# Two small tiles of a block-attention and mixture-of-experts kernel are made wider

## Chip, cores and metric

The kernel runs on one core of a Trainium2 chip. The metric is the device time of one execution in microseconds (us); the time before is the median of three runs. The five engines are TensorE (PE, its weight loads listed apart as PEld), VectorE (DVE), ScalarE (ACT), GpSimd (POOL) and SyncE (SP, which issues DMAs).

## What is computed

Block-causal attention (4 batches, 8 heads, 576 tokens, head size 64, blocks of 64), and behind it a mixture of four experts over the 2304 tokens, all in float32:

```python
scores = scale * np.matmul(q, k.transpose(0, 1, 3, 2))
mask = block_i >= block_j
scores = np.where(mask, scores, -1000000000.0)
attn = softmax of scores over the keys
x = (attn @ v), laid out as (2304, 512)
p = domain_probs / (domain_probs.sum(-1, keepdims=True) + 1e-09)
for e in range(4):
    h = np.maximum(x @ w1[e], 0.0)          # 512 -> 1024
    out += p[:, e:e + 1] * (h @ w2[e])      # 1024 -> 512
```

## The kernel before

The 2304 tokens are cut into five blocks: the first 64 tokens of all four batches (256), then the other 512 of each batch. A small planner in the kernel (`Flow`) gives every operation an engine, a cost in ns and a due time, and writes the program out in the order that it finds; the costs depend on sizes and engines alone, not on addresses.

To keep float32 precision every operand of a large product is split in two, a high part and the rest (`w1h`/`w1l`, `w2h`/`w2l`, `xh`/`xl`, `hh`/`hl`), and a product is three matmuls: high by high, rest by high, high by rest, each with its own weight load, 128 rows by 512 columns (256 for the first block).

- **First stage**, up to about 565 us: attention (scores at L521 and L522 from `KK`, `HH`, `LL`; the sums with `v` at L733 from `VN` and `S`) is worked in between the expert layers of the first three blocks. There the first layer is L1013 (`mm1`, moving `xh` or `xl`, stationary `w1h` or `w1l`) and the second L1063 (`mm2`, moving `w2h` or `w2l`, stationary `hh` or `hl`): 96 chunks, 12 first-layer matmuls each, and 960 matmuls of the second layer.
- **Last stage**, from about 565 us: the last two blocks go together through seven products instead of eight for each pair of chunks (`product`, L1236; moving are `xh`, `xl` and the sums `S1` to `S4` and `A22`, each with its high and rest part), ScalarE takes copies of products out of PSUM (L1256), and the second layer is L1299 (`mm2_half`).

All tiles lie one behind the other in each SBUF partition, in the order in which they are declared. The pool "const" holds what lives throughout: the weights' and activations' splits `w1h` ... `w2l`, `hh`, `hl`, `xh`, `xl`, the raw weights, and at its end `ident`, `probs_n` and `probs_s` (L284 to L287). The pool "attn" follows: `kr`, `qr`, `kT`, `qT`, `KK`, `HH`, `LL`, `VN`, `tr`, `tc`, then `S`, `cm`, `mx`, `sa`, `sb`, `xs`, `rc` (L289 to L310). Before the last stage "attn" is closed and the pool "pair" takes its place, from the same byte (L1114 to L1140): `A22`, `S2`, `S3`, `S1`, `S4`, more buffers for `hh`, `hl`, `w1h`, `w1l`, `w2h`, `w2l`, `w1r`, `o`, and `sc`. In a trace these buffers carry a p at the end of their names (`w2hp`, `hhp`, `scp`); `xh` and `xl` serve as `hh` and `hl` buffers too in this stage, as slices of a "const" tile.

The first tile, `w1h`, begins at byte 16,512 of the partition, which is 128 modulo 256. Every tile that TensorE reads is a multiple of 256 bytes long, and so are most others; `probs_n` has 320 bytes, `probs_s` 128, `tc` 64. So the offsets modulo 256 are:

```
                                   before
"const" tiles that TensorE reads      128
"attn": kr ... tr (KK, HH, LL, VN)     64     from byte 128,576
"attn": S ... rc                      128     from byte 170,880
"pair": all tiles                      64     from byte 128,576
```

Of the kernel before, what the change touches and what calls it, by code (L numbers as in the profile page):

```python
# [8 lines left out]
F32 = mybir.dt.float32  # L9
# [201 lines left out]
def kernel(  # L211
# [14 lines left out]
    P = 128  # L226
# [33 lines left out]
    MAXW = max(j[2] - j[1] for j in every)  # L260
# [3 lines left out]
    const = ctx.enter_context(tc.tile_pool(name="const", bufs=1))  # L264
# [4 lines left out]
    def bufs(tag, n, shape, dt=F32, pool=const):  # L269
        fl.add_bufs(tag, [pool.tile(shape, dt, name=f"{tag}{i}") for i in range(n)])  # L270
# [13 lines left out]
    XR = [const.tile([P, KC, MAXW], F32, name=f"xr{g}") for g in range(2)]  # L284
    ident = const.tile([P, P], F32, name="ident")
    probs_n = const.tile([P, len(BLOCKS) * 4, E], F32, name="probs_n")
    probs_s = const.tile([P, 32], F32, name="probs_s")  # L287
    const.seal()
    attn = short.enter_context(tc.tile_pool(name="attn", bufs=1))  # L289
    for tag, n, shape, dt in (  # L290
        ("kr", 2, [P, S], F32),
        ("qr", 1, [P, 2 * MAXW], F32),
        ("kT", 1, [P, S], F32),
        ("qT", 1, [P, 2 * MAXW], F32),
        ("KK", 2, [P, 2 * S], F32R),
        ("HH", 1, [P, 2 * MAXW], F32R),
        ("LL", 1, [P, 2 * MAXW], F32R),
        ("VN", 2, [P, (MASK_BLOCK + MAXW) // P + 1, 3, D], F32),
        ("tr", 1, [P, MAXW], F32),
        ("tc", 1, [P, MAXW // 32], F32),  # L300
        ("S", 2, [P, 2 * MAXC], F32),
        ("cm", 1, [P, 2 * MAXW], F32),
        ("mx", 1, [P, 2 * MAXW], F32),
        ("sa", 1, [P, 2 * MAXW], F32),
        ("sb", 1, [P, 2 * MAXW], F32),
        ("xs", 1, [P, MAXW], F32),
        ("rc", 1, [P, MAXW], F32),
    ):
        bufs(tag, n, shape, dt, attn)
        counts[tag] = n  # L310
# [1082 lines left out]
```

## Time and profile before

| | us |
|---|---|
| median of three runs | 908.78 (908.73 to 908.81) |
| the profiled execution, its own time | 909.63 |
| its span, first to last instruction | 907.6 |

The mean granted clock of TensorE over the span is 0.997. The profile lists an instruction as "line engine op out<-moving,stationary" for a matmul (the first name behind the arrow is what streams, the second what stands in the array); "128\*128 128x512 f32" is its shape. Matmuls are pipelined and the profile models their ends, so a matmul's duration is longer than the distance from its start to the next one's; the start times are what was recorded.

### The profile page before, as it was taken

Reading aid. Unit: us, or ns where it says so; the run is one execution under the profiler, and the core shown is the slowest. Engines: PE = TensorE matmul, PEld = TensorE weight load, DVE = VectorE, ACT = ScalarE, POOL = GpSimd, SP = SyncE. Lnnn points to the kernel's source line nnn. Section 1 sums busy time; section 2 is a strip of 40 time slices with the busy share of each in tenths; the row PEclk is TensorE's granted clock in tenths of the full one; section 3 lists DMA queues with packets and bytes.
Section 4 is the critical chain, followed back from the end, with each engine's and each line's share of the span. In section 5 each row is a group of like instructions: output and inputs, shape, how many; then the busy total and the mean of one; then the engine's idle time right before and its main releaser. Section 6 shows DMA issues by size and latency. Waiting matters only on the chain.

```text
span 907.6 us, 12364 instructions
## 1 busy us (share of the span) xinstructions
PE 896.4 (99%) x4302; PEld 714.6 (79%) x4302; DVE 692.5 (76%) x1298; ACT 451.3 (50%) x857; POOL 140.5 (15%) x53
## 2 busy tenths in 40 slices
PE   8999999999999999999999999899999999999998
PEld 4777888787877877787787787688888888888886
DVE  6799999888988988988988788965565655666532
ACT  3587766564646556557654643554343333333220
POOL 1101110422233142224232322000000000000000
PEclk9999999999999999999999999999999999999999
DMA  9875558455435345644444232312021212110002
GB/s 181 169 206 167 151 130 188 146 121 113 122 88 137 98 126 109 176 117 106 109 105 130 72 106 80 117 47 66 27 70 37 69 42 63 48 47 24 12 1 93
DMA packets 214654, 91.17 MB, mean 100 GB/s; under 512 B 130368, under 2 KB 195904, under 8 KB 214592
## 3 DMA queue, kind: packets, MB, share of 16 engines
q1 hardware_dynamic: 211424, 89.59, 38.0%
q10 hardware_dynamic: 3168, 0.79, 0.5%
q8 instruction: 34, 0.56, 0.3%
q14 instruction: 28, 0.23, 0.1%
HBM read 85.63 MB, written 4.72 MB: 100 GB/s over the span
## 4 chain that ended last, share of the span: by engine, by line
PE 92%; DVE 3%; DMA 2%; SPq 1%; ACT 0%; issue 0%; DVEq 0%; ACTq 0%
PE h L1013 23%; PE acc L1063 23%; PE acc L1299 20%; PE h L1236 9%; PE att L1236 7%; PE att L733 4%; PE att L521 2%; PE att L522 2%; SPq L339 1%; PE acc L733 1%; PE att L509 1%; DMA S<-in_v_dram 1%; DVE xr L352 1%; PE acc L509 1%; DMA probs_n<-in_moe_domain_probs_dram 0%; DMA cm<-in_q_dram 0%
## 5 line engine op out<-in xcount | busy, mean ns | idle before, releaser
L1013 PE MATMUL h<-xl,w1h 128*128 128x512 f32 (+1 forms) x384 | 136.5, 355 | 1.8 <-DVE xl L352 1.8
L1013 PE MATMUL h<-xh,w1h 128*128 128x512 f32 (+1 forms) x384 | 137.7, 359 | 0.0
L1013 PE MATMUL h<-xh,w1l 128*128 128x512 f32 (+1 forms) x384 | 136.6, 356 | 0.0
L1063 PE MATMUL acc<-w2h,hh 128*128 128x512 f32 x316 | 125.2, 396 | 0.0
L1063 PE MATMUL acc<-w2l,hh 128*128 128x512 f32 x316 | 123.5, 391 | 0.0
L1063 PE MATMUL acc<-w2h,hl 128*128 128x512 f32 x316 | 123.3, 390 | 0.0
L345 ACT CAST w2h<-w2r 128x512 fp32r<-128x512 f32 x113 | 70.3, 622 | 69.2 <-PE acc L1063 56.8
L666 POOL PARTITION_ALL_REDUCE sb<-sa x24 | 80.4, 3398 | 136.6 <-DVE sa L352 102.3
L687 POOL PARTITION_ALL_REDUCE mx<-cm x16 | 56.0, 3497 | 274.1 <-DVE cm L352 238.3
L352 DVE TENSOR_TENSOR w1l<-w1r,w1h 128x512 fp32r<-128x512 f32 (+1 forms) x124 | 86.7, 699 | 1.6 <-ACT w1h L345 0.6
L1030 ACT ACTIVATE hh<-h 128x512 fp32r<-128x512 f32 (+1 forms) x95 | 49.8, 525 | 72.1 <-PE h L1013 71.9
L352 DVE TENSOR_TENSOR w2l<-w2r,w2h 128x512 fp32r<-128x512 f32 x117 | 79.7, 682 | 4.9 <-ACT w2h L345 4.6
L1013 PEld LDWEIGHTS h<-xl,w1h 128*128 128x128 f32 x384 | 72.9, 190 | 12.6 <-DVE xl L352 2.2
L1013 PEld LDWEIGHTS h<-xh,w1h 128*128 128x128 f32 x384 | 72.9, 190 | 11.7 <-issue 1.2
L1013 PEld LDWEIGHTS h<-xh,w1l 128*128 128x128 f32 x384 | 72.9, 190 | 10.5
L345 ACT CAST w1h<-w1r 128x512 fp32r<-128x512 f32 (+1 forms) x111 | 66.1, 596 | 17.5 <-DMA w1r<-in_moe_w_dram 9.6
L1063 PEld LDWEIGHTS acc<-w2h,hl 128*128 128x128 f32 x316 | 59.3, 188 | 13.1
L1063 PEld LDWEIGHTS acc<-w2h,hh 128*128 128x128 f32 x316 | 59.5, 188 | 12.8 <-issue 1.7
L345 ACT COPY S<-att 128x512 f32<-128x512 f32 (+2 forms) x95 | 50.9, 536 | 34.4 <-DVE att L591 24.2
L1063 PEld LDWEIGHTS acc<-w2l,hh 128*128 128x128 f32 x316 | 59.5, 188 | 10.4
L1032 DVE SCALAR_TENSOR_TENSOR hl<-h,hh 128x512 fp32r<-128x512 f32 (+1 forms) x95 | 56.2, 591 | 10.5 <-ACT hh L1030 10.1
L352 DVE TENSOR_TENSOR S<-S,mx 128x1024 f32<-128x1024 f32 (+4 forms) x80 | 59.9, 792 | 3.2 <-POOL mx L687 3.0
(331 smaller groups left out, 1823.0 us busy)
## 6 DMA issues: line engine op xcount, KB each, us to landing
w2r<-in_moe_w_dram SPq DMA_DIRECT2D x128, 256.0 KB, 3.0
w1r<-in_moe_w_dram SPq DMA_DIRECT2D x120, 256.0 KB, 3.0
qr<-in_q_dram SPq DMA_DIRECT2D x112, 64.0 KB, 2.9
kr<-in_k_dram SPq DMA_DIRECT2D x64, 72.0 KB, 3.4
VN<-in_v_dram SPq DMA_DIRECT2D x32, 128.0 KB, 2.5
out_dram<-o SPq DMA_DIRECT2D x12, 256.0 KB, 2.1
w1rp<-in_moe_w_dram SPq DMA_DIRECT2D x8, 256.0 KB, 2.9
out_dram<-op SPq DMA_DIRECT2D x4, 256.0 KB, 2.0
```

The costliest lines, as they stand in the source:

```text
L345: o = op(engs, 0, lambda e: nc.scalar.copy(dst, src) if e == "act" else nc.vector.tensor_copy(dst, src), r, u, prio)
L352: o = op(engs, 0, lambda e: ENG[e].tensor_tensor(out=dst, in0=a, in1=b, op=alu), r, u, prio)
L509: nc.tensor.matmul(out=o, lhsT=KK.tile[hp, k0:k0 + n], rhs=qT.tile[hp, lo:W], start=True, stop=True)
L666: sums.append((yield op("pool", 150 + 6.3 * W, lambda _, h=h: nc.gpsimd.partition_all_reduce(sb.tile[:, h * W:h * W + W], sa.tile[:, h * W ...
L687: lambda _: nc.gpsimd.partition_all_reduce(mx.tile[:, :2 * W], src, P, RED.max),
L733: nc.tensor.matmul(out=x.tile[64 * g:64 * g + 64, W - w:W], lhsT=lhsT, rhs=rhs, start=(i == 0), stop=(i == len(todo) - 1))
L1013: nc.tensor.matmul(out=ps[:, :n], lhsT=s.tile[:, ks], rhs=x.tile[:, kc, :n], start=(kc == 0 and m == 0), stop=(kc == KC - 1 and m == 2),)
L1030: a = yield op("act", 0.833 * n + 55, lambda _: nc.scalar.activation(hh.tile[:, :n], ps[:, :n], AF.Relu), [mm], [pb, hh], 0.0)
L1032: l = yield op("dve", 1.04 * n + 70, lambda _: nc.vector.scalar_tensor_tensor(out=hl.tile[:, :n], in0=ps[:, :n], scalar=0.0, in1=hh.tile[: ...
L1063: nc.tensor.matmul(out=acc, lhsT=s.tile[:, ts], rhs=w.tile, start=(f == 0 and m == 0), stop=(f == FC - 1 and m == 2))
L1236: nc.tensor.matmul(out=ps[:, :n], lhsT=w.tile[:, ks], rhs=x[:, kc, :n], start=(start and kc == 0 and m == 0), stop=(i in (2, 3, 4) and kc ...
L1299: nc.tensor.matmul(out=acc, lhsT=s.tile[:, ts], rhs=w.tile, start=(c == 0 and x == 0), stop=(c == 3 and x == 2))
```

## The change

`probs_s` gets 48 columns instead of 32, and `tc` MAXW // 8 = 64 columns instead of 16. Both are read and written in the same slices as before; nothing else differs.

```diff
     probs_n = const.tile([P, len(BLOCKS) * 4, E], F32, name="probs_n")
-    probs_s = const.tile([P, 32], F32, name="probs_s")
+    probs_s = const.tile([P, 48], F32, name="probs_s")
     const.seal()
...
         ("tr", 1, [P, MAXW], F32),
-        ("tc", 1, [P, MAXW // 32], F32),
+        ("tc", 1, [P, MAXW // 8], F32),
         ("S", 2, [P, 2 * MAXC], F32),
```

## Rows read from the trace of the kernel before

**Rows 1.** The page: busy time of each engine, and the chain that ended last

```profile
PE 896.4 (99%) x4302; PEld 714.6 (79%) x4302; DVE 692.5 (76%) x1298; ACT 451.3 (50%) x857; POOL 140.5 (15%) x53
...
PE 92%; DVE 3%; DMA 2%; SPq 1%; ACT 0%; issue 0%; DVEq 0%; ACTq 0%
```

**Rows 2.** Stages from 565 us: busy PE, PEld, DVE, ACT, POOL; clock, DMA, GB/s

```profile
565.00:582.00 17.00, 14.38 (x61) 10.80 (x60) 17.00 (x25) 8.06 (x13) 0.00 (x0) 1.00 0.32 108
582.00:700.00 118.00, 118.00 (x512) 95.80 (x511) 72.83 (x132) 49.13 (x86) 0.00 (x0) 1.00 0.19 56
...
800.00:896.00 96.00, 96.00 (x418) 78.23 (x417) 48.46 (x81) 26.90 (x46) 0.00 (x0) 1.00 0.09 28
```

**Rows 3.** PE groups, 560 to 908 us: count | busy us, mean ns | idle before

```profile
L1299 PE MATMUL acc<-w2h,hhp 128*128 128x512 f32 x80 | 31.5, 394 | 0.0
...
L1299 PE MATMUL acc<-w2h,hlp 128*128 128x512 f32 x80 | 31.3, 392 | 0.0
...
L1299 PE MATMUL acc<-w2l,xh 128*128 128x512 f32 x60 | 23.5, 391 | 0.0
L1299 PE MATMUL acc<-w2lp,xh 128*128 128x512 f32 x44 | 17.4, 395 | 0.0
...
L1236 PE MATMUL att<-xh,w1hp 128*128 128x512 f32 x24 | 9.5, 394 | 0.0
...
L1299 PE MATMUL acc<-w2hp,hhp 128*128 128x512 f32 x24 | 9.4, 391 | 0.0
...
L1236 PE MATMUL att<-xh,w1l 128*128 128x512 f32 x24 | 9.3, 389 | 0.0
...
L1299 PE MATMUL acc<-w2hp,hh 128*128 128x512 f32 x20 | 7.9, 394 | 0.0
...
L1236 PE MATMUL h<-S3l,w1h 128*128 128x512 f32 x16 | 6.3, 396 | 0.0
...
L1236 PE MATMUL h<-A22h,w1h 128*128 128x512 f32 x16 | 6.3, 394 | 0.0
...
L1236 PE MATMUL h<-S3l,w1hp 128*128 128x512 f32 x16 | 6.3, 392 | 0.0
```

**Rows 4.** Timeline of PE near the end: start us, duration us, what

```profile
887.08 0.39 PE L1299 MATMUL acc<-w2h,xh 128*128 128x512 f32 x1
...
889.80 0.39 PE L1299 MATMUL acc<-w2hp,xh 128*128 128x512 f32 x1
...
892.60 0.39 PE L1299 MATMUL acc<-w2h,xh 128*128 128x512 f32 x1
...
900.78 0.39 PE L1299 MATMUL acc<-w2hp,hhp 128*128 128x512 f32 x1
...
903.28 0.39 PE L1299 MATMUL acc<-w2hp,hlp 128*128 128x512 f32 x1
```

**Rows 5.** The chain that ended last, in order of time: start, length us

```profile
583.77 7.00 PE h L1236 x30
```

**Rows 6.** Weight loads, 560 to 908 us: count | busy us, mean ns | idle

```profile
L1299 PEld LDWEIGHTS acc<-w2l,xh 128*128 128x128 f32 x60 | 11.3, 188 | 2.5
...
L1299 PEld LDWEIGHTS acc<-w2lp,xh 128*128 128x128 f32 x44 | 8.3, 188 | 1.9
```

**Rows 7.** DVE groups, 560 to 908 us: count | busy us, mean ns | idle

```profile
L352 DVE TENSOR_TENSOR w2l<-w2r,w2h 128x512 fp32r<-128x512 f32 x20 | 13.7, 687 | 4.2 <-ACT w2h L345 4.2
...
L352 DVE TENSOR_TENSOR w2lp<-w2r,w2hp 128x512 fp32r<-128x512 f32 x11 | 7.6, 688 | 7.0 <-ACT w2hp L345 6.9
```

**Rows 8.** One PE group, in 150 to 300 us and in 549 to 565 us

```profile
L1063 PE MATMUL acc<-w2l,hh 128*128 128x512 f32 x91 | 35.5, 390 | 0.0
...
L1063 PE MATMUL acc<-w2l,hh 128*128 128x512 f32 x12 | 4.7, 389 | 0.0
```

**Rows 9.** PE groups by shape, 60 to 545 us

```profile
L733 PE MATMUL att<-S,VN 128*64 128x448 f32 x52 | 12.0, 539 | 0.0
...
L733 PE MATMUL att<-S,VN 128*64 128x320 f32 x52 | 9.2, 432 | 0.0
```

## Prediction

> **What bounds the kernel now.** I read the busy times and the chain of waits first. TensorE is busy 99% of the span and carries 92% of the chain that ended last [rows 1]: nothing else has to get faster for the end to move, and no other engine can hide a gain of TensorE for long. Then the stage table. From 582 us on TensorE is busy for the whole of each stretch, at a granted clock of 1.00 (its 2.4 GHz level), while DVE, ACT and the DMA share fall off [rows 2]. Only 565 to 582 us has gaps (14.38 us busy of 17.00). So in the last third the time is the number of matmuls times the distance from one start to the next, and the question is what sets that distance.
>
> The distance can be read from start times. In the quiet end of the kernel twelve matmuls that read `w2h`/`w2l` against `xh`/`xl` start at 887.08 and the next group starts at 889.80: 2.72 us, 226.7 ns each. The next twelve, of the same shape, line and stationary tiles but with `w2hp`/`w2lp` moving, take 889.80 to 892.60: 2.80 us, 233.3 ns each. Nothing waits in either. Twelve more with both operands in p-tiles run from 900.78; the twelfth starts at 903.28, so 2.50 us over eleven, 227.3 ns [rows 4]. The chain of waits has a longer run of the slow kind at 583.77, thirty matmuls in 7.00 us, 233.3 ns each, these of the `S2` and neighbouring tiles against `w1h`/`w1l` [rows 5].
>
> The group table of the stage shows that this is general. A matmul's modelled duration moves with that distance, so the differences of the means count, not the means: `w2lp` against `xh` 395 ns, `w2l` against `xh` 391; `w2h` against `hhp` 394 and against `hlp` 392; `w2hp` against `hhp` 391; `S3l` against `w1h` 396, against `w1hp` 392; `xh` against `w1hp` 394, against `w1l` 389 [rows 3]. The slow ones are those whose two operands come from different pools. By the allocation, all tiles of the pool "const" begin at 128 modulo 256, and those of the pools "attn" up to `tc` and "pair" at 64. So **the pairs that cost more are those whose moving and stationary tile stand at different offsets modulo 256**. Equal offsets, 64 with 64 or 128 with 128, cost the same within about 1 ns.
>
> **What the change does, part by part.** `probs_s` grows from 128 to 192 bytes per partition: everything after it moves up by 64, so `kr` to `tr` and, later, all "pair" tiles go from 64 to 128. `tc` grows from 64 to 256 bytes: `S` to `rc` move by 256 in all and stay at 128. The two tiles are read and written in the same slices, so no instruction, wait, DMA or byte is added, removed or reordered; the planner's costs don't see an address. Only the offsets change.
>
> Now the sum, by classes of the two lines of the last stage, L1236 with 672 and L1299 with 768 matmuls. Their counts are those of the groups [rows 3]:
> - Moving at 64, stationary at 128: on L1299 three groups of 44 and three of 20, on L1236 24 groups of 16 or 8, 288 in all (`S3l` and `A22h` against `w1h` stand for them, 396 and 394). Together 480. Price of one: 4 ns by the means (395 against 391) to 6.6 ns by the quiet end (233.3 against 226.7). I take 5, nearer to the means, since they hold the whole stage with its other engines' traffic: 480 x 5 = 2.4 us (1.9 to 3.2).
> - Moving at 128, stationary at 64: on L1299 three groups of 80, on L1236 96 in six groups (one stands there, 394 against 389 with `w1l`). Together 336. Price 1 to 5 ns by these rows (392 and 394 against 391, 394 against 389), I take 2.5: 0.84 us (0.3 to 1.7).
> - Both at 64: 72 on L1299 and 192 on L1236, 264. Price 0 to 1 ns (391 and 392 against 391), I take 0.5: 0.13 us (0 to 0.26).
> - Both at 128 already: 360, nothing.
>
> That is 3.4 us. The 61 matmuls in 565 to 582 us [rows 2] are in these counts, and there TensorE stands waiting for ACT's copies of its own products, so what it saves is partly waited away: at 5 ns on about 40 of them, 0.2 us off. Left: **3.2 us**.
>
> The cover of a gain: who could become late next? In 582 to 896 us no stretch has idle TensorE, and DVE is busy 72.83 of 118.00 us in the first of these stretches and 48.46 of 96.00 in the last [rows 2]; a stage that runs 1% faster asks 1% more of engines that are a third idle. The output after the last matmul stays as long as it is.
>
> The weight loads aren't what is slow: 188 ns for one from `xh` under moving `w2lp` and 188 under `w2l` [rows 6]. VectorE doesn't see the offset either: its subtraction into `w2lp` takes 688 ns, into `w2l` 687 [rows 7]. So I cost the edit at nothing for the other engines.
>
> Before 565 us the two layers' 2,112 matmuls (by the loops) read "const" tiles alone and stay where they are. The attention's score products have both operands at 64 and will have both at 128: equal before and after, 0. Its products with `VN` (64) against `S` (128) are an unequal pair, in 4-byte float: between 320 and 448 columns their mean grows by 539 - 432 = 107 ns [rows 9], which is two cycles a column at 2.4 GHz with no excess that these rows can show. I take 0; at the quiet end's 6.6 ns for each of 160 pairs that run side by side it would be 1.1 us, which goes to the second rival below.
>
> The profiled execution took 909.63 us (span 907.63), 0.85 us over the median; the terms are differences and carry over. 908.78 - 3.2 = **905.6 us**; an execution like the profiled one would have a span near 904.4.
>
> **The rule that speaks against it.** The rows show 6.6 ns between two runs that differ in the moving tile's pool alone [rows 4]. The Trainium skill, page "TensorE: Matmul & The Clock Gate", section "Step-by-step: what each phase is for", has two independent read ports of SBUF, one for the moving operand and one for the weights, so that loading the next weights takes nothing from the running matmul. By it no pair of offsets could cost anything, and the sum would be 0 instead of 3.2 us. The trace differs: the price hangs on the pair, since `w2hp` moving is slow against `xh` and not against `hhp` [rows 3].
>
> **The rivals.**
> *Nothing changes (908.8 us).* Pool and offset go together in the kernel before, so the price may belong to where the pools lie, low and high in the partition, or to how these tiles are filled, and the offset is only its mark. Then all stays. For it: no row has a "const" tile at 64. Against it: `A22h` begins at byte 128,576, right behind the last "const" tile, and against `w1h` costs the same 394 ns as `w2hp`, 64 KB further up, does against `hh` [rows 3]; and `w2h` and `xh`, both "const" and some 40 to 60 KB apart, run at 226.7 ns [rows 4], so distance alone costs nothing. The Trainium skill's two read ports, above, would end here as well. To the same end leads that the allocator rounds sizes so that nothing moves; its tile of 64 bytes moved `S` by just 64, which speaks against it.
> *More than forecast (902.7 us).* Every matmul reaches the quiet end's pace: 480 x 6.6 + 336 x 4 + 264 x 2 = 5.0 us, and `VN` pairs give 1.1. Against it: equal pairs of the stage itself stand at 391 beside 389 in quieter stretches.
> *Slower (914 us).* What costs may be the coincidence of offsets between TensorE's reads and what VectorE, ScalarE and the DMAs do at the same time. Then moving the attention's tiles onto 128 puts them where the 2,112 early matmuls read. At the 4 ns of the means that is 8.4 us, less 3.2: 914. It decides from 3.2/2,112 = 1.5 ns on. Against it: those engines walk through whole tiles and pass every offset, and early groups run at 390 ns beside the attention's work and at 389 after it has ended [rows 8], so all they cost now is about 1 ns.
>
> **How the numbers follow.** Forecast 0.78, more than forecast 0.05, nothing changes 0.13, slower 0.04. The forecast's own terms, low and high, add to 2.0 and 5.0 us: 903.8 to 906.8; widened by 0.3 for the difference between executions (the profiled one stands 0.85 from the median, the three runs within 0.08 of each other) that is 903.5 to 907.1, and with the nearer half of the second case it holds 8 in 10. A change of 0.2% (1.8 us, 907.0) is about what can be told from none. Faster by more: nearly all of the forecast and the second case, 0.80; within: 0.15; slower: 0.05.
>
> **What would show it.** Right: `w2lp` against `xh` and `S3l` against `w1h` fall from 395 and 396 to 391 or less; `w2h` against `hhp` from 394 to 391; the twelve of `w2hp` against `xh` near the end take 2.72 us instead of 2.80; the stage from 582 us to the last matmul is 3 us shorter; weight loads stay at 188, subtractions at 687; the stretch up to 565 us ends within 0.5 us of where it did. Wrong: p-tile groups keep 394 to 396 (place, not offset), or the early groups rise above 390 (coincidence with the other engines), or TensorE shows idle time after 582 us.

## The result, and the profile after

The changed kernel takes 902.38 us (median of six), the kernel before 909.08 beside it: 6.7 us less, and the ratio of the two is 0.9916 (95% interval 0.9906 to 0.9926). The forecast was 905.6 us with a range of 903.5 to 907.1. The direction and the mechanism were right; the gain was twice the forecast of 3.2 us, and the time lies below the range. The rival "more than forecast" (902.7), which had been given a chance of 0.05, names the time that came.

The profiled execution after took 903.51 us, its span 901.6. The page: busy times, and the chain that ended last.

```profile
PE 890.2 (99%) x4302; PEld 715.3 (79%) x4302; DVE 692.3 (77%) x1298; ACT 451.8 (50%) x857; POOL 140.6 (16%) x53
...
PE 93%; DVE 3%; DMA 2%; SPq 1%; issue 0%; ACT 0%; DVEq 0%; ACTq 0%
```

The same 4,302 matmuls, and 6.2 us less of busy TensorE than in [rows 1]; every other engine is as busy as before. Where the time went is seen in the groups of the last stage, 560 to 908 us (count | busy us, mean ns | idle before):

```profile
L1299 PE MATMUL acc<-w2h,hhp 128*128 128x512 f32 x80 | 31.1, 389 | 0.0
...
L1299 PE MATMUL acc<-w2l,xh 128*128 128x512 f32 x60 | 23.3, 389 | 0.0
L1299 PE MATMUL acc<-w2lp,xh 128*128 128x512 f32 x44 | 17.1, 389 | 0.0
...
L1299 PE MATMUL acc<-w2hp,hhp 128*128 128x512 f32 x24 | 9.3, 389 | 0.0
...
L1236 PE MATMUL att<-xh,w1l 128*128 128x512 f32 x24 | 9.3, 389 | 0.0
...
L1236 PE MATMUL h<-S3l,w1h 128*128 128x512 f32 x16 | 6.2, 389 | 0.0
```

Beside [rows 3] the reader is to see two things. The unequal pairs fell from 394 to 396 ns, as forecast. But the equal ones fell too: `w2l` against `xh`, both at 128 in either kernel, from 391 to 389, and `w2hp` against `hhp` from 391 to 389. All stand now at the one value that `xh` against `w1l` had in the kernel before.

The weight loads are untouched, as in [rows 6]:

```profile
L1299 PEld LDWEIGHTS acc<-w2l,xh 128*128 128x128 f32 x60 | 11.3, 188 | 2.3
...
L1299 PEld LDWEIGHTS acc<-w2lp,xh 128*128 128x128 f32 x44 | 8.3, 188 | 1.7
```

The timeline gives the length of the last stage. Before, its first matmul on L1236 starts at 564.95 and its last on L1299 at 903.28 [rows 4]: 338.3 us.

```profile
564.95 0.39 PE L1236 MATMUL att<-xh,w1h 128*128 128x512 f32 x1
```

After:

```profile
564.71 0.39 PE L1236 MATMUL att<-xh,w1h 128*128 128x512 f32 x1
...
883.88 0.39 PE L1299 MATMUL acc<-w2hp,xh 128*128 128x512 f32 x1
...
886.60 0.39 PE L1299 MATMUL acc<-w2h,xh 128*128 128x512 f32 x1
...
897.25 0.39 PE L1299 MATMUL acc<-w2hp,hlp 128*128 128x512 f32 x1
```

That is 332.5 us, 5.8 less, and the twelve of `w2hp` against `xh` take 886.60 - 883.88 = 2.72 us, where [rows 4] had 2.80. The stage before it saved 0.9 us (below). 5.8 + 0.9 is the whole difference of the medians.

### The profile page after: what moved, and what is told of

Its sections match the earlier page's. It is cut to its first block, busy times and chain, and to the rows that moved or that the text cites. A ratio compares the mean times of both kernels' runs of the same rounds, so it can differ in the third digit from the quotient of the medians.

```text
span 901.6 us, 12364 instructions
## 1 busy us (share of the span) xinstructions
PE 890.2 (99%) x4302; PEld 715.3 (79%) x4302; DVE 692.3 (77%) x1298; ACT 451.8 (50%) x857; POOL 140.6 (16%) x53
## 4 chain that ended last, share of the span: by engine, by line
PE 93%; DVE 3%; DMA 2%; SPq 1%; issue 0%; ACT 0%; DVEq 0%; ACTq 0%
PE h L1013 24%; PE acc L1063 23%; PE acc L1299 19%; PE h L1236 9%; PE att L1236 7%; PE att L733 4%; PE att L521 2%; PE att L522 2%; PE att L509 1%; PE acc L733 1%; DMA w1r<-in_moe_w_dram 1%; SPq L339 1%; DMA S<-in_v_dram 1%; PE acc L509 1%; DVE xr L352 1%; DMA cm<-in_q_dram 0%
## 5 line engine op out<-in xcount | busy, mean ns | idle before, releaser
L1013 PE MATMUL h<-xl,w1h 128*128 128x512 f32 (+1 forms) x384 | 136.5, 356 | 1.9 <-DVE xl L352 1.9
L1013 PE MATMUL h<-xh,w1h 128*128 128x512 f32 (+1 forms) x384 | 137.5, 358 | 0.0
L1013 PE MATMUL h<-xh,w1l 128*128 128x512 f32 (+1 forms) x384 | 136.5, 355 | 0.0
L1063 PE MATMUL acc<-w2h,hh 128*128 128x512 f32 x316 | 125.1, 396 | 0.0
L1063 PE MATMUL acc<-w2l,hh 128*128 128x512 f32 x316 | 123.4, 391 | 0.0
L1063 PE MATMUL acc<-w2h,hl 128*128 128x512 f32 x316 | 123.2, 390 | 0.0
L1013 PEld LDWEIGHTS h<-xl,w1h 128*128 128x128 f32 x384 | 73.1, 190 | 12.4 <-DVE xl L352 2.1
L1013 PEld LDWEIGHTS h<-xh,w1h 128*128 128x128 f32 x384 | 72.9, 190 | 11.6 <-issue 1.2
L1013 PEld LDWEIGHTS h<-xh,w1l 128*128 128x128 f32 x384 | 73.0, 190 | 10.3
L1063 PEld LDWEIGHTS acc<-w2h,hl 128*128 128x128 f32 x316 | 59.3, 188 | 13.0
L1063 PEld LDWEIGHTS acc<-w2h,hh 128*128 128x128 f32 x316 | 59.5, 188 | 12.7 <-issue 1.7
L1063 PEld LDWEIGHTS acc<-w2l,hh 128*128 128x128 f32 x316 | 59.5, 188 | 10.3
```

The source lines that it names most:

```text
L1013: nc.tensor.matmul(out=ps[:, :n], lhsT=s.tile[:, ks], rhs=x.tile[:, kc, :n], start=(kc == 0 and m == 0), stop=(kc == KC - 1 and m == 2),)
L1063: nc.tensor.matmul(out=acc, lhsT=s.tile[:, ts], rhs=w.tile, start=(f == 0 and m == 0), stop=(f == FC - 1 and m == 2))
```

## The experiments

The theory after this result: a matmul whose moving and stationary tiles begin at different offsets modulo 256 is slow, and the equal ones that follow it are slow for a while too. The rivals: the offset itself (128 good, 64 bad); the place of the pools; the tiles from `S` on, which `tc` moves; other engines at work on tiles at 64.

Single executions of one kernel differ by up to 5.7 us (the kernel before, 907.67 to 913.36 in the 25 executions beside e5 to e7), and in the profiles the same matmul near 80 us starts anywhere between 78.2 and 81.5. Behind that point the stretches of kernels with the same distances between their tiles repeat to less than 0.1 us, so beside the time the table gives two stretches from the start times of each profile: from one first-layer matmul near 80 us (L1013) to the first matmul on L1236, and from there to the last on L1299. Each ratio is to executions of the kernel before taken beside the run (medians 910.12 us for e1 to e4, 909.67 for e5 to e7).

| kernel | offsets modulo 256 | time, us | ratio to before | near 80 us to L1236 | last stage |
|---|---|---|---|---|---|
| before | const 128, attn and pair 64 | 909.08 | | 485.42 | 338.34 |
| after | all 128 | 902.38 | 0.9916 | 484.49 | 332.54 |
| e1_probs_only | all 128, `S` to `rc` 192 | 903.29 | 0.9926 (0.9911 to 0.9941) | 484.49 | 332.59 |
| e2_tc_only | as before, `S` to `rc` 64 | 911.08 | 1.0009 (0.9999 to 1.0018) | 485.45 | 338.42 |
| e3_all_at_64 | all 64 | 903.53 | 0.9934 (0.9917 to 0.9950) | 484.49 | 332.59 |
| e4_w2_at_64 | as after, const `w2h`, `w2l` 64 | 913.26 | 1.0035 (1.0024 to 1.0047) | 490.33 | 336.98 |
| e5_pair_32 | as after, pair 160 | 909.65 | 1.0000 (0.9985 to 1.0015) | 484.49 | 339.19 |
| e6_pair_64 | as after, pair 192 | 909.03 | 0.9981 (0.9968 to 0.9994) | 484.49 | 338.35 |
| e7_pair_128 | as after, pair 0 | 908.14 | 0.9981 (0.9967 to 0.9996) | 484.49 | 338.34 |
| e8_w2p_only | as after, `w2hp`, `w2lp` 64 | 904.58, one execution | | 484.49 | 335.15 |
| e9_pair_256 | as after, pair 128 (384 modulo 512) | 902.58, one execution | | 484.49 | 332.53 |
| e10_w1p_only | as after, `w1hp`, `w1lp` 64 | 905.38, one execution | | 484.49 | 333.18 |

From the matmul near 80 us on, all of them have the same matmuls in the same order; only addresses differ. The unused tiles that make the distance are declared on the lines that are there already, so line numbers stay.

**Each half of the change alone.**

```diff
-    probs_s = const.tile([P, 32], F32, name="probs_s")
+    probs_s = const.tile([P, 48], F32, name="probs_s")
```

> One part alone: probs_s is widened, tc is not. The attention's tiles up to tr and all pair tiles go to 128 modulo 256, S to rc go to 192. Theory (the price lies on matmuls whose moving and stationary tile differ in offset, and equal pairs that follow them pay too): the whole gain, 902.4 us give or take 0.5, with every group of the last stage at 389 ns; S at 192 against VN at 128 costs nothing, since these products showed no price at 128 against 64 either. Rival (the price lies on S, sa and their neighbours): less than half of the gain, 906 or more.

```diff
-        ("tc", 1, [P, MAXW // 32], F32),
+        ("tc", 1, [P, MAXW // 8], F32),
```

> The other part alone: tc is widened, probs_s is not. S to rc go to 64, everything else stays as in the kernel before. Theory of the pair: no gain, 909 us, p-tile groups against const tiles at 394 to 396 ns as before. Rival (S, sa and neighbours carry the price): a gain of 3 us or more.

The first has the whole gain, both stretches to 0.05 us; the second has none. So `S` and its neighbours carry nothing: at 192 against `VN` at 128 (e1) or at 64 against 64 (e2) the stretches don't move. The change would have done with its first line.

**All at 64.** In the changed kernel:

```diff
-    bufs("w1h", 4, [P, DM], F32R)
+    const.tile([P, 48], F32, name="pad0"); bufs("w1h", 4, [P, DM], F32R)
```

> The changed kernel with 192 unused bytes ahead of the first tile: every tile that TensorE reads begins at 64 modulo 256 instead of 128. Theory of the pair: only the difference counts, so 902.4 us as the changed kernel, 389 ns throughout the last stage. Rival (the offset itself counts, 64 is the bad one): all 3,500 matmuls of the expert layers pay at least the 3 ns that pairs of 64 with 64 paid in the last stage of the kernel before (229.6 ns from start to start against 226.7), more than 10 us, 912 or more.

Both stretches are those of the changed kernel. The groups, 560 to 908 us:

```profile
L1299 PE MATMUL acc<-w2h,hhp 128*128 128x512 f32 x80 | 31.1, 389 | 0.0
...
L1299 PE MATMUL acc<-w2lp,xh 128*128 128x512 f32 x44 | 17.1, 389 | 0.0
...
L1236 PE MATMUL h<-S3l,w1h 128*128 128x512 f32 x16 | 6.2, 389 | 0.0
```

64 isn't a bad offset; what counts is that the two are equal. It also settles what the price of pairs 64 with 64 was in the kernel before: not theirs, but their neighbours'.

**Const tiles made unequal.** In the changed kernel:

```diff
-    bufs("w2h", 4, [P, DM], F32R)
+    const.tile([P, 48], F32, name="pad0"); bufs("w2h", 4, [P, DM], F32R)
     bufs("w2l", 4, [P, DM], F32R)
-    bufs("w1r", 3, [P, KC, P])
+    const.tile([P, 16], F32, name="pad1"); bufs("w1r", 3, [P, KC, P])
```

> The changed kernel with w2h and w2l of the const pool alone at 64 modulo 256 (192 unused bytes ahead of them, 64 behind), all else at 128. Theory of the pair: the second layer of the first three blocks, 960 matmuls that were fast in both kernels, becomes unequal and pays 6.6 ns each, 6.3 us; the first-layer groups behind them pay some 20 ns each for the way back, about 1.3 us; in the last stage 504 matmuls with w2h or w2l moving pay 3.3 us and their followers 0.5: 913.8 us, L1063 at 395 ns or more. Rival (the price belongs to where the pools lie in the partition, not to the offset): nothing, 902.4.

The time is 913.26 us, slower than the kernel before. The second layer of the first three blocks, fast in both kernels (390 ns in [rows 8]), became slow, and the first layer behind it too, whose own tiles had not moved (389 in the changed kernel). The groups of 300 to 450 us, and the second of them in the changed kernel:

```profile
L1063 PE MATMUL acc<-w2l,hh 128*128 128x512 f32 x92 | 36.3, 395 | 0.0
...
L1013 PE MATMUL h<-xl,w1h 128*128 128x512 f32 x89 | 34.8, 391 | 0.0
```

```profile
L1013 PE MATMUL h<-xl,w1h 128*128 128x512 f32 x92 | 35.8, 389 | 0.0
```

The stretch from 80 us to L1236 is 5.8 us longer than in the changed kernel, the last stage 4.4 us (expected 3.8). The first part fell short: 870 of the 960 second-layer matmuls lie in that stretch, and they take 4.6 us more, 5.3 ns each and not 6.6, the first layer 1.1 us more. Beside e1 and e3 (903.29 and 903.53), which run as the changed kernel does, 913.26 us is some 9.9 us more where 11.4 were expected, so that the nearness to 913.8 is partly luck. The place of a pool is out all the same: these are const tiles, low in the partition.

**How far apart.** In the changed kernel, an unused tile of 8, 16, 32 or 64 floats ahead of the pair pool:

```diff
-        more = ctx.enter_context(tc.tile_pool(name="pair", bufs=1, reuse_waits="tile"))
+        more = ctx.enter_context(tc.tile_pool(name="pair", bufs=1, reuse_waits="tile")); more.tile([P, 8], F32, name="pad0")
```

> The changed kernel with 32 unused bytes ahead of the pair pool: all tiles of the pair pool at 160 modulo 256, the const tiles at 128, a difference of 32. Theory (any difference of the two operands costs): unequal pairs at 233 ns from start to start and their followers slowed, the last stage as long as in the kernel before, 908 to 909 us. Rival (the price grows with the difference): about half of it, 905.5.

> The same with 64 unused bytes: pair tiles at 192, const tiles at 128, a difference of 64 in the other direction than in the kernel before. Theory: as the kernel before, 908 to 909 us. Rival (only tiles that begin below the other's offset pay): 902.4.

> The same with 128 unused bytes: pair tiles at 0, const tiles at 128 modulo 256. If what counts is the offset modulo 256: unequal pairs at 233 ns, 908 to 909 us. If it is the offset modulo 128, or 64: 902.4 us as the changed kernel, 389 ns throughout the last stage.

> The changed kernel with 256 unused bytes ahead of the pair pool: pair tiles at 384 modulo 512, const tiles at 128, equal modulo 256 and unequal modulo 512. If what counts is the offset modulo 256: the last stage as in the changed kernel, 332.5 us from its first to its last matmul, 389 ns throughout. If it is modulo 512 or more: 338 us as in the kernel before.

The last stage is 339.2, 338.4 and 338.3 us at distances of 32, 64 and 128 bytes, and 332.5 at 256. The price doesn't grow with the distance, it is paid to either side, and equality modulo 256 is enough to be rid of it. One group of this view in 560 to 908 us, at 32, at 128 and at 256 bytes:

```profile
L1299 PE MATMUL acc<-w2lp,xh 128*128 128x512 f32 x44 | 17.4, 395 | 0.0
```

```profile
L1299 PE MATMUL acc<-w2lp,xh 128*128 128x512 f32 x44 | 17.3, 394 | 0.0
```

```profile
L1299 PE MATMUL acc<-w2lp,xh 128*128 128x512 f32 x44 | 17.1, 389 | 0.0
```

At 64 bytes the equal length of the stage hides a change: the two unequal classes have changed places. In the kernel before, where the pair tiles lie 64 below the const tiles, the mean distance from start to start is 233.2 ns for a pair tile moving against a const tile and 230.9 ns the other way round; in e6, where they lie 64 above, it is 230.9 and 233.2. At 32 bytes both are at 233 (233.0 and 233.1), which is most of the 0.8 us by which that stage is longer than in the kernel before; at 128 bytes, where above and below are the same modulo 256, both are at 232.4 to 232.5. So at a distance of 64 the price depends on the side: a moving tile 64 below its stationary tile costs more than one 64 above.

**One unequal moving tile, and who pays behind it.** In the changed kernel:

```diff
-        add("w2h", 2, [P, DM], F32R)
+        more.tile([P, 48], F32, name="pad0"); add("w2h", 2, [P, DM], F32R)
         add("w2l", 2, [P, DM], F32R)
-        add("w1r", 1, [P, KC, P])
+        more.tile([P, 16], F32, name="pad1"); add("w1r", 1, [P, KC, P])
```

> The changed kernel with w2hp and w2lp alone at 64 modulo 256, all else at 128: 264 matmuls of the last stage have an unequal moving tile, in runs of twelve. Theory: these at 233 ns, and the first six equal matmuls behind each run carry about 21 ns together (steps of 226, 235 to 237, 227 to 229, 231 to 233, 230 to 231 and 227 to 228 ns as behind such runs in the kernel before), everything further from them at 226 to 227: 264 x 6.6 + 22 x 21 ns = 2.2 us over the changed kernel. Rival (the slow equal pairs of the kernel before come from other engines at work on tiles at 64): equal matmuls behind the runs at 227 from the first on, 1.7 us.

The last stage is 2.6 us longer than in the changed kernel, more than the 2.2 expected. The expectation had counted the runs wrong: the 264 matmuls stand in 42 runs of 3 to 12, not in 22 of twelve, and behind each of the 41 that have followers the same six steps come, 20 ns over the pace together. 264 x 6.6 ns and 41 x 20 ns are 2.6 us. The timeline of TensorE near the end (start us, duration us, what) around one run of twelve:

```profile
884.12 0.39 PE L1299 MATMUL acc<-w2h,xh 128*128 128x512 f32 x1
884.34 0.39 PE L1299 MATMUL acc<-w2l,xh 128*128 128x512 f32 x1
884.57 0.39 PE L1299 MATMUL acc<-w2h,xl 128*128 128x512 f32 x1
884.79 0.39 PE L1299 MATMUL acc<-w2hp,xh 128*128 128x512 f32 x1
...
887.60 0.39 PE L1299 MATMUL acc<-w2h,xh 128*128 128x512 f32 x1
887.82 0.40 PE L1299 MATMUL acc<-w2l,xh 128*128 128x512 f32 x1
888.06 0.39 PE L1299 MATMUL acc<-w2h,xl 128*128 128x512 f32 x1
888.28 0.40 PE L1299 MATMUL acc<-w2h,xh 128*128 128x512 f32 x1
888.52 0.39 PE L1299 MATMUL acc<-w2l,xh 128*128 128x512 f32 x1
888.75 0.39 PE L1299 MATMUL acc<-w2h,xl 128*128 128x512 f32 x1
888.98 0.39 PE L1299 MATMUL acc<-w2h,xh 128*128 128x512 f32 x1
```

The twelve unequal ones take 887.60 - 884.79 = 2.81 us, 234 ns each. The six equal ones behind them take 888.98 - 887.60 = 1.38 us, 230 ns each; six of the undisturbed pace would take 1.36. In single ns the steps behind the run are 226, 235, 229, 232, 231, 227, and then 226 to 227 on end: the six steps together are 20 ns over the pace. The three ahead of the run stand at it. Nothing else works on tiles at 64 in this stretch but the writers of `w2hp` and `w2lp`, the last of which ends at 868.5 us, so the followers' price comes from TensorE's own past: the rival of the other engines falls.

It was in the trace of before as well, in the rows right behind 892.60 of [rows 4]:

```profile
892.83 0.40 PE L1299 MATMUL acc<-w2l,xh 128*128 128x512 f32 x1
893.06 0.39 PE L1299 MATMUL acc<-w2h,xl 128*128 128x512 f32 x1
893.29 0.40 PE L1299 MATMUL acc<-w2h,xh 128*128 128x512 f32 x1
893.52 0.39 PE L1299 MATMUL acc<-w2l,xh 128*128 128x512 f32 x1
893.75 0.39 PE L1299 MATMUL acc<-w2h,xl 128*128 128x512 f32 x1
893.98 0.39 PE L1299 MATMUL acc<-w2h,xh 128*128 128x512 f32 x1
```

Six steps of the equal pair from 892.60 to 893.98 are 1.38 us here too.

**One unequal stationary tile.** In the changed kernel:

```diff
-        add("w1h", 2, [P, DM], F32R)
+        more.tile([P, 48], F32, name="pad0"); add("w1h", 2, [P, DM], F32R)
         add("w1l", 2, [P, DM], F32R)
-        add("w2h", 2, [P, DM], F32R)
+        more.tile([P, 16], F32, name="pad1"); add("w2h", 2, [P, DM], F32R)
```

> The changed kernel with w1hp and w1lp alone at 64 modulo 256 (the tiles behind them moved by 256): 288 matmuls of the last stage have an unequal stationary tile, 48 runs of six, between equal ones. If a stationary tile at another offset costs what the long run of such matmuls near the end of the kernel before showed (229, 231 to 232 and 226 ns in turn behind equal ones, and nothing behind it): 288 x 2.3 ns = 0.7 us over the changed kernel's 332.5 us for the stage. Rival (it costs what a moving tile costs, and the same way back behind it): 288 x 6.6 + 48 x 21 ns = 2.9 us.

The last stage is 0.64 us longer, as the small price has it. One run of six in its timeline, between equal ones:

```profile
705.22 0.39 PE L1236 MATMUL h<-S1h,w1hp 128*128 128x512 f32 x1
...
706.59 0.39 PE L1299 MATMUL acc<-w2h,hhp 128*128 128x512 f32 x1
...
707.95 0.39 PE L1236 MATMUL h<-A22h,w1hp 128*128 128x512 f32 x1
```

1.37 us for the six unequal ones and 1.36 for the six equal ones behind them: 2.3 ns each, nothing carried over. In the kernel before the same kind of pair cost 4 ns on the mean, because it often came behind pairs of the other kind. There the steps stay at 233 to 234 ns, as in these six, which have only pairs of their own kind between them and a run of `w2hp` against `hh` that ended at 652.8 us:

```profile
655.60 0.40 PE L1236 MATMUL att<-xh,w1hp 128*128 128x512 f32 x1
...
657.00 0.40 PE L1299 MATMUL acc<-w2h,hhp 128*128 128x512 f32 x1
```

Is it the stationary tile's being the odd one that makes the price small? e8 and e10 differ in a second thing: in e8 the moving tile lies 64 below its stationary tile, in e10 64 above. The trace of e6 has them the other way round. Twelve of `w2h` against `hhp` and `hlp`, moving 64 below because the pair tiles are up at 192, and the last nine of a run of `w2hp` against `xh`, moving 64 above:

```profile
881.06 0.40 PE L1299 MATMUL acc<-w2h,hhp 128*128 128x512 f32 x1
...
883.86 0.40 PE L1299 MATMUL acc<-w2h,hhp 128*128 128x512 f32 x1
...
890.11 0.39 PE L1299 MATMUL acc<-w2hp,xh 128*128 128x512 f32 x1
...
892.17 0.40 PE L1299 MATMUL acc<-w2h,xh 128*128 128x512 f32 x1
```

2.80 us for twelve is 233 ns each, and 2.06 us for nine is 229: `w2hp` moving, costly in [rows 4], has become the cheap kind, and `w2h` against `hhp` the costly one. So the steady price goes by the side and not by which of the two tiles is the odd one. What comes ahead and behind does not follow the side alone: the first three of that run of `w2hp` take 237, 235 and 231 ns, and the ten equal ones behind it 50 ns over the pace together, where nothing followed in e10.

## Why the prediction was wrong, point by point

**What bounds the kernel** was right: TensorE carries 91 to 94% of the chain that ended last in every kernel here, no other engine hid or took back any of the gain, and the last stage fell by what its matmuls fell.

**Which matmuls pay** was right, and now shown: the pair's inequality, not the place (e4), not the offset itself (e3), not other engines (e8). "Modulo 256", read from the allocation alone, is what e7 and e9 bear out. That the price also depends on which of the two lies below (e6) the prediction did not say; its two unequal classes are the two sides.

**The price was mis-sized, in all four classes for one reason: the base.** The prediction took 391 ns, the mean of the equal pairs in the same stage, as what a matmul costs when nothing is wrong, and set "both at 128 already: 360, nothing". Those equal pairs were mixed in between unequal ones and carried part of their price. The free value was 389: it stood in [rows 3] for `xh` against `w1l`, and in [rows 8] for a stretch without p-tiles. The spread of the group, which the prediction did not weigh, says so. Duration of `w2l` against `xh`, minimum/median/maximum, before and after:

```profile
L1299 PE MATMUL acc<-w2l,xh x60: 387/389/398, 607.4 to 897.6; 128*128 128x512 f32 x60
```

```profile
L1299 PE MATMUL acc<-w2l,xh x60: 389/389/389, 606.7 to 891.6; 128*128 128x512 f32 x60
```

A median of 389 under a mean of 391 is a group of undisturbed matmuls and some late ones. A base of 389 raises each class's price by 2 ns, to 7, 4.5, 2.5 and 2 ns; the distances below give 6.5, 4.2, 2.7 and 1.9. They are the mean distances from start to start of the kernel before, less the 226.7 to 226.8 ns at which all stand after; six steps of 0.3 to 1.8 us, in which TensorE waits, are left out and have their own line.

| class of pair, moving/stationary | count | forecast, us | distance before, ns | worked out, us |
|---|---|---|---|---|
| 64/128 | 480 | 2.4 | 233.2 | 3.1 |
| 128/64 | 336 | 0.84 | 230.9 | 1.4 |
| 64/64 | 264 | 0.13 | 229.4 | 0.7 |
| 128/128 | 360 | 0 | 228.6 | 0.7 |
| waits of 565 to 582 us | | -0.2 | | -0.1 |
| sum | | 3.2 | | 5.8 |

The stage gave 5.8. The waits grew from 4.82 to 4.91 us, so that term was near. The 0.7 us that each equal class gave back lay outside the forecast's bounds (0 to 0.26, and 0). For the 64/128 pairs the step that failed is "I take 5, nearer to the means": the quiet end's 6.6 was the price, and the means were low only because their base was high.

**The stage before** was costed at 0 and gave 0.9 us (485.42 to 484.49), with `KK`, `HH` and `LL` at 64 beside const tiles at 128. Those products are equal pairs in either kernel, but in the kernel before they stand between equal pairs of the other offset. Some got faster themselves, the 320-column ones for one. By shape, 60 to 545 us, in the kernel before and after:

```profile
L522 PE MATMUL att<-LL,KK 128*128 128x320 f32 x24 | 7.5, 311 | 0.0
```

```profile
L522 PE MATMUL att<-LL,KK 128*128 128x320 f32 x24 | 7.4, 308 | 0.0
```

Of the 0.93 us 0.27 lie on the score products and 0.66 on the expert layers around them, by the start times. The first eleven expert matmuls behind a score product account for 0.69 us, and the 1,161 that stand further from one got 0.03 us slower: it is the price of followers again, which the prediction had put at nothing. That a matmul also pays when only its neighbour stands at another offset fits e2 (485.45, with `KK` to `LL` at 64) and e3 (484.49, all at 64), but no run moved these tiles alone, so this split is argued. The sign "the stretch up to 565 us ends within 0.5 us of where it did" came true (564.95 and 564.71) by luck: the first 80 us happened to take 0.7 us longer in the profiled execution after.

**`VN` against `S`** was rightly taken at 0: 539 and 432 ns [rows 9] are 539 and 432 after, and e1 and e2 move `S` without effect. So the rival "more than forecast" had the right time by partly wrong terms: its 1.1 us for `VN` did not come, and 0.9 came from the border instead. The argument against it, "equal pairs of the stage itself stand at 391 beside 389 in quieter stretches", read the symptom as a cost of the surroundings.

**The other rivals.** "Slower" did not happen: in 300 to 450 us the early groups of L1063 stand where they stood or 1 ns lower (`w2l` against `hh` 390 before, 389 after). "Nothing changes" fell with the result, and its reason, the place of the pools, with e3 and e4. The rule of the Trainium skill, page "TensorE: Matmul & The Clock Gate", section "Step-by-step: what each phase is for", that loading the next weights takes nothing from the running matmul, doesn't cover this case as it stands: the weight loads keep their 188 ns, but the matmul's pace hangs on where the weights lie relative to the moving tile. e3 and e4 measure that, and the measurement decides.

## What to carry to other kernels

Where float32r matmuls (the type of the split tiles, F32R in the diffs) have a weight load each, put all tiles that they read, moving and stationary, at the same offset modulo 256: two helper tiles of 320 and 128 bytes at the end of one pool moved the next pools by 192 modulo 256 and cost this kernel 0.7%. When an effect is priced by comparing groups of one stage, look at the spread and not only the mean of the group that is taken as free, and take the base from a stretch that has none of the effect: neighbours may carry part of it. Here the quiet stretch that shows the price clean was a better guide (6.6 ns, 6.5 measured) than the stage's means.

## What the runs showed of the hardware that was not expected

- With equal offsets a matmul of 512 columns in these float32r products, each with its own weight load, starts every 226.7 ns at a granted clock of 1.00, whatever the offset (e3), the place and the other engines' work (after the change, with VectorE 63% busy in 582 to 700 us as with 50% in 800 to 890). The Trainium skill's page "TensorE: Matmul & The Clock Gate", section "Wait — 56ns, not 53.3ns?", gives 215.7 ns for 512 columns back to back. The bf16 matmuls of L364 early in the kernel before agree with it, though they have a weight load each too (215 ns from 7.13 to 7.34 us, 216 at 5.83, 11.74 and 18.79 us); the equal float32r pairs do not get below 226.7 on the mean in any run. What makes the 11 ns between the two was not tested.
- The steady price goes by the side: 6.6 ns for each matmul whose moving tile lies 64 below its stationary tile (e8, e6's `w2h` against `hhp`), 2.3 ns where it lies 64 above (e10, e6's `w2hp` against `xh`), about 6 ns at 32 and 128 bytes to either side (e5, e7). At 64 above, the pairs stay at 233 ns behind a run of the costly kind. The 4-byte float products of `S` with `VN` showed no price at a distance of 64 (e1).
- Behind a run of the costly kind in e8 the six equal matmuls are 20 ns late together, in a fixed pattern (226, 235, 229, 232, 231, 227, to 1 ns behind each of 41 runs). Behind the cheap kind it is nothing in e10 and 50 ns in e6's run. Which buffer or port makes it was not found: only starts were measured, and the weight loads' 188 ns don't show it.
